# Reordered reads and weight splits in a gated attention kernel: the first tile's x on two queues, the border's x pieces in threes and twos

## The chip, the cores and the metric

The kernel runs on one core of a Trainium2 chip. The metric is the device time of one execution in microseconds (us), lower is better. Three timed runs of the kernel before gave 1965.87, 1967.68 and 1967.72 us; their median is 1967.68 us.

## What is computed

The reference takes x (2048 rows of 640), a key and a value cache of 32 heads (the last 512 positions of 128 are used), and weights in float32. It normalizes x, runs attention and a two-layer network on the same normalized rows, and gates the one with the other:

```python
xn = _layernorm(x, axis=-1)
s = _A_ref(xn, A_k_cache, A_v_cache, A_wq, A_wo)      # q = xn @ wq, softmax(q k^T / sqrt(128)) v, @ wo
g = _silu(_B_ref(xn, B_w1, B_b1, B_w2, B_b2))         # relu(xn @ w1 + b1)**2 @ w2 + b2
return x + s * g
```

The inner size of the network is 1728, that is 13 chunks of 128 and one of 64.

## The kernel before

Each float32 operand of a product is split into a high part (a rounded copy, made on ScalarE) and a low part (operand minus high part, made on VectorE or GpSimd), and each product of two operands takes three matmuls: high by high, high by low, low by high. "Preparing" a weight below means making these two parts.

**Tiles and stages.** The 2048 rows are four tiles of 512 columns (NT). In the first stage three tiles run through the network, one chunk f of its inner size after the other: `up` (L400), or `up_half` (L377) for the chunk of 64, makes one chunk of the hidden layer, and `down` (L426) adds its product with w2 to five banks of PSUM. The chunks are reordered so that the one of 64 stands at place rp = 3. The gates and the transposed normalized x are written to memory. In the second stage the 32 heads are worked off in 128 units: a half `hf` (two tiles), a group `g` of two heads, a tile t of the half, a head j of the group. Four units (UPG) make a group. The last tile's network follows behind the last units.

**The first tile.** `ln_first` (L208) normalizes the first 512 rows in four blocks of 128. SyncE (SP) issues the four reads of x (L222 to L225), then those of the first weights (`load_part`, L330), of the biases into `br`, and of the weights of chunks 1 and 2. Meanwhile TensorE runs WARM = 36 transposes of a constant (L242). For each block VectorE takes statistics (`bn`, two halves, then `aggr`); ScalarE takes roots (`root`), centres and scales the blocks; VectorE takes the reciprocal of the root, and GpSimd finishes that of the first two blocks (`newton(0)`). TensorE transposes the scaled blocks into `px` (`turn`), ScalarE and VectorE copy them to the two parts of `xT`, and `up` begins. `raws` holds the raw weights of chunk 0.

**Order within a chunk.** The engines work in the order in which the code records instructions. In tile 0, `square_split` (L369) squares the hidden chunk on GpSimd and then prepares w1 of chunk f + 1 (`split_w`, L359) ahead of splitting the hidden chunk itself.

**The order of the second stage** is a plan written out by hand: `at(when, f, ...)` (L964) notes a step with a due time, and L1150 records all steps sorted by time. A unit has PERIOD = 12.4 of that scale. The steps of a unit i that matter here:

- `s_mm` makes the scores in four banks `s`; `max_fold` and `gather` (three small ScalarE copies, at 3.95) and `row` (at 4.1) find the maximum of each column. `row` writes it as `rowm` to memory (`m_d`) and reads it back to all 128 partitions (`bm`), both DMAs on SP's queue, and the second is issued only when the first has landed.
- `shift` (at 10.4) subtracts `bm` from the four banks into `e` on VectorE, which frees the banks for the next unit's scores; `expo` and `p_hi` (ScalarE) and `p_lo` (GpSimd) make the parts `pt` for `v_mm`, the product with v.
- The sums take the same way back through `s_d` and `bs`.
- `r_mm` multiplies the outcome of both heads (`ot`) with wo into a running sum.
- Four weights of each group (q, k, v, o) are loaded into a raw tile, one of each kind, by `load_raw` on SP's queue and prepared by `prep` (ScalarE then GpSimd) one period later. L972 to L977 give the due times; each load is due 10.5 ahead of its own prep.
- At the border between the two halves, the second half's x is read: two tiles of ten pieces of 256 KB each (`load_xT`, L546; parts 0 and 1 of five chunks), at the times of X_AT (L984 to L994), all on ScalarE's DMA queue, over tiles that the first half's units have used.

In the notes below unit numbers count from 0; 64 is the first unit of the second half. L73 in the profile is the line of a helper that records most instructions, so the profile is read by tile names.

Of the kernel before, what the change touches and what calls it, by code (L numbers as in the profile page):

```python
# [14 lines left out]
P = 128  # L15
NT = 512
EPS = 1e-5
WARM = 36


@with_exitstack
def kernel(
# [15 lines left out]
    S, D = x.shape  # L38
# [3 lines left out]
    NB = NT // P  # L42
# [159 lines left out]
    def biases():  # L202
# [2 lines left out]
        dve.tensor_copy(b1_sb, pb[:, :FC])  # L205
        dve.tensor_copy(b2_sb, pb[:, 32 : 32 + DC])

    def ln_first():  # L208
        mv = xp.tile([P, 4, NB], F32, tag="mv", name="mv0")
        sc = xp.tile([P, 3, NB], F32, tag="sc", name="sc0")  # L210
# [5 lines left out]
        pool.memset(warm, 1.0)  # L216
        eps = mv[:, 3, 1:2]
        dve.memset(eps, EPS)
        act.activation(warm, warm, AF.Sqrt)
        hd = D // 2  # L220
        xn = []
        for b in range(NB):  # L222
            xb = ln_tile(0, b)
            sp.dma_start(xb, x[b * P : (b + 1) * P, :])
            xn.append(xb)  # L225
        br = xp.tile([P, P], F32, tag="br", name="br", bufs=1)
        dve.memset(br, 0.0)
        BR.append(br)
        for k in range(2):
            load_part(0, k)  # L230
        raws = [PRE[0, k] for k in range(2)]
        for lo, hi in ((0, rp), (rp, rp + 1), (rp + 1, FC)):
            f0, m = chunks[lo][0], chunks[lo][1]
            sp.dma_start(
                br[lo:hi, :m], b1[f0 : f0 + m * (hi - lo)].rearrange("(f p) -> f p", p=m)
            )
        sp.dma_start(br[32 : 32 + DC, :], b2.rearrange("(c p) -> c p", p=P))
        for f in (1, 2):
            for k in range(2):
                load_part(f, k)  # L240
# [11 lines left out]
        def aggr(b):  # L252
            dve.bn_aggr(mv[:, :2, b], sts[b])
# [29 lines left out]
        for b in range(n):  # L283
            for i in range(2):
                bn(b, i)
            aggr(b)
        centre(0)
        root(0)
        centre(1)
# [37 lines left out]
        for i in range(2):  # L327
            pool.dma_start(xT_d[t][i][:, cs, :], raw(xs[i])[:, cs, :])

    def load_part(f, k):  # L330
        f0, n = chunks[f]
        if f % 3 and f < 9:
            if k == 0:
                BOTH[f] = keep.tile([P, 2, D], F32, tag="acc", name=f"wr{f}", bufs=2)
            w = BOTH[f][:, k, :]
        else:
            w = xp.tile([P, D], F32, tag="stw", name=f"w{k + 1}r{f}", bufs=2)
        if k == 0:
# [30 lines left out]
    def square_split(t, f, r, hi, lo):  # L369
        g, a, v = engines(t)  # L370
        g.tensor_tensor(r, r, r, op=ALU.mult)
        if t == 0 and f:
            split_w(f + 1, 0)
        a.activation(hi, r, AF.Copy)
        v.tensor_tensor(lo, r, raw(hi), op=ALU.subtract)

    def up_half(t, f, xs):  # L377
        n = chunks[f][1]
        ph = ps_h.tile([P, NT], F32, tag="ph", name=f"ph{t}_{f}")
        w = w1s[f][0]  # L380
        order = [(c, i) for c in range(DC - 1) for i in range(2)] + [(DC - 1, 1), (DC - 1, 0)]
        for k, (c, i) in enumerate(order):
            m = n if i else 2 * n
            nc.tensor.matmul(
                ph[:m, :],
                w[:, c, :m],
                xs[i][:, c, :],
                start=k == 0,
                stop=k == len(order) - 1,
            )  # L390
        r = hp.tile([P, NT], F32, tag="r", name=f"r{t}_{f}")[:n, :]
        g, a, v = engines(t)
        a.activation(r, ph[n : 2 * n, :], AF.Copy)
        v.tensor_tensor(r, ph[:n, :], r, op=ALU.add)
        a.activation(r, r, AF.Relu, bias=b1_sb[:n, f : f + 1])
        h = hp.tile([P, NT], F32R, tag="h0", name=f"h{t}_{f}")
        square_split(t, f, r, h[:n, :], h[n : 2 * n, :])
        return h

    def up(t, f, xs):  # L400
        if chunks[f][1] < P:
            return up_half(t, f, xs)
        ph = ps_h.tile([P, NT], F32, tag="ph", name=f"ph{t}_{f}")
        if t == 0 and f < 2:
            order = [(c, i, j) for c in range(3) for i, j in ((0, 0), (0, 1))]
            order += [(0, 1, 0), (1, 1, 0), (3, 0, 0), (3, 0, 1), (2, 1, 0), (3, 1, 0)]
            order += [(4, 0, 0), (4, 1, 0), (4, 0, 1)]
        else:
            order = [(c, i, j) for c in range(DC) for i, j in ((0, 0), (0, 1), (1, 0))]
        for k, (c, i, j) in enumerate(order):  # L410
            nc.tensor.matmul(  # L411
                ph,
                w1s[f][i][:, c, :],
                xs[j][:, c, :],
                start=k == 0,
                stop=k == len(order) - 1,
            )
            if t == f == 0 and k == 9:
                biases()
        r = hp.tile([P, NT], F32, tag="r", name=f"r{t}_{f}")  # L420
        engines(t)[1].activation(r, ph, AF.Relu, bias=b1_sb[:, f : f + 1])
        hs = [hp.tile([P, NT], F32R, tag=f"h{i}", name=f"h{t}_{f}_{i}") for i in range(2)]
        square_split(t, f, r, hs[0], hs[1])
        return hs
# [542 lines left out]
    for n in range(HALF * NG):  # L967
        hf, g = divmod(n, NG)
        base = UPG * PERIOD * n
        for j in range(G):  # L970
            h = g * G + j
            for kind, when in (  # L972
                ("q", (j - 1 - AHEAD) * PERIOD + 8.4),
                ("k", (j - 2) * PERIOD + 8.5),
                ("v", j * PERIOD + 8.4),
                ("o", (j if n == 0 else -j) * PERIOD + 8.5),
            ):  # L977
                if n or kind in "vo":
                    at(base + when - 10.5, load_raw, kind, hf, h)
                    at(base + when, prep, kind, hf, h)  # L980
    at(10.0, pad, pools["ep"], 480)
    for t in range(TPH):
        w = (NG * UPG + t * G - 5) * PERIOD
        X_AT = [(11.65, 2)]  # L984
        for k in (1, 2):
            X_AT += [(k * PERIOD + 3.97, 2), (k * PERIOD + 7.85, 1)]
            X_AT += [(k * PERIOD + 11.65, 2)] * (k == 1)
        pieces = [(c, i) for c in range(DC) for i in range(2)]
        for k, (when, n) in enumerate(X_AT):
# [208 lines left out]
```

## Time and profile before

| what | value |
|---|---|
| time, median of three runs (lowest to highest) | 1967.68 us (1965.87 to 1967.72) |
| profiled execution, its own time | 1966.04 us |
| span of its program | 1964.2 us |
| mean granted TensorE clock | 0.998 |
| busy VectorE, ScalarE, GpSimd | 78%, 60%, 70% |
| DMA | 218.97 MB, mean 111 GB/s |

In a timeline row the first number is the start in us from the begin of the span, the second the duration, then come engine, line, operation, output<-inputs, shapes, the count of merged instructions, and in brackets the idle time of the engine just before, with what ended it. PE is TensorE's matmul, PEld its load of weights, DVE is VectorE, ACT ScalarE, POOL GpSimd; SPq and ACTq are the queues on which SyncE and ScalarE issue DMAs. A row of the windows view gives, for one stretch, its length, the busy time and count of each engine, the granted TensorE clock, the DMA share, and GB/s.

### The profile page before, as it was taken

To read this page: it belongs to the slowest core of one execution; us is meant where nothing else is said; L and a number is where in the kernel's file an instruction comes from. 1 tells how busy PE (TensorE), PEld (TensorE's weight loads), DVE (VectorE), ACT (ScalarE), POOL (GpSimd) and SP (SyncE) were. 2 spreads that over 40 slices of the span, in tenths; PEclk is the share of its full clock that TensorE was granted. 3 is DMA by queue.
4 is the path that set the end of the run, shared out by engine and by line. 5 is a ranking of instruction groups with operands and counts; after the bars stand their busy time and mean duration, and the time that the engine had idled before them with its cause. 6 is when DMAs were issued, how large, how long until landed. Compare 5 with 4: busy or idle time off the path is not lost. (4 is left out here: it accounts for less than half of the span.)

```text
span 1964.2 us, 25621 instructions
## 1 busy us (share of the span) xinstructions
PE 1952.7 (99%) x8612; PEld 1612.2 (82%) x8612; DVE 1535.0 (78%) x2640; ACT 1186.1 (60%) x2038; POOL 1375.1 (70%) x757
## 2 busy tenths in 40 slices
PE   9999999999999999999999999999999999999998
PEld 7888888888888888888887888888888888888887
DVE  5633337788888888888888878888888888888865
ACT  4432326766666666666666676666666666666643
POOL 2121226888878888888887888888888888888841
PEclk9999999999999999999999999999999999999999
DMA  5330453333333322222235433333333333323253
GB/s 181 95 118 28 182 198 128 97 92 92 92 92 92 92 92 93 92 91 94 90 95 181 133 119 108 113 113 113 113 113 113 113 113 114 97 92 92 86 187 118
DMA packets 127594, 218.97 MB, mean 111 GB/s; under 512 B 23420, under 2 KB 37542, under 8 KB 126182
## 3 DMA queue, kind: packets, MB, share of 16 engines
q1 hardware_dynamic: 121718, 197.67, 33.1%
q0 software_dynamic: 2864, 14.42, 1.8%
q10 hardware_dynamic: 2880, 5.24, 0.9%
q8 instruction: 67, 1.10, 0.2%
q14 instruction: 65, 0.53, 0.1%
HBM read 193.41 MB, written 23.87 MB: 111 GB/s over the span
## 5 line engine op out<-in xcount | busy, mean ns | idle before, releaser
L73 POOL TENSOR_TENSOR pt<-e,pt 128x1024 fp32r<-128x1024 f32 x256 | 615.2, 2403 | 125.6 <-ACT pt L73 99.1
L73 PE MATMUL r<-ot,wo 128*128 128x512 f32 x1920 | 496.7, 389 | 0.0
L73 PE MATMUL pq<-ax,wq 128*128 128x512 f32 x1920 | 456.1, 389 | 0.0
L73 PEld LDWEIGHTS pq<-ax,wq 128*128 128x128 f32 x1920 | 360.4, 188 | 75.2 <-DVE q L73 0.4
L73 PEld LDWEIGHTS r<-ot,wo 128*128 128x128 f32 x1920 | 360.4, 188 | 74.9
L73 PE MATMUL o<-pt,wv 128*128 128x512 f32 x1536 | 370.6, 390 | 0.2
L73 PE MATMUL s<-q,wk 128*128 128x512 f32 x1536 | 369.4, 389 | 1.1 <-DVE e L73 1.1
L73 ACT ACTIVATE e<-e 128x1024 f32<-128x1024 f32 x256 | 269.6, 1053 | 135.1 <-DVE e L73 110.2
L73 DVE TRANSPOSE_TENSOR_REDUCE rdm<-s 128x16 f32<-128x512 f32 x512 | 344.3, 709 | 6.3 <-PE s L73 6.3
L73 PEld LDWEIGHTS s<-q,wk 128*128 128x128 f32 x1536 | 288.1, 188 | 62.2 <-DVE e L73 2.4
L73 PEld LDWEIGHTS o<-pt,wv 128*128 128x128 f32 x1536 | 287.9, 188 | 62.0 <-POOL pt L73 2.6
L73 DVE TENSOR_TENSOR e<-s,bm 128x512 f32<-128x512 f32 x512 | 312.7, 666 | 16.6 <-DMA bm<-m_d 16.2
L73 POOL TENSOR_TENSOR su<-e,e 128x1024 f32<-128x1024 f32 x128 | 308.7, 2412 | 0.0
L73 ACT ACTIVATE pt<-e 128x1024 fp32r<-128x1024 f32 x256 | 271.9, 1062 | 8.2 <-ACT rdm L73 1.2
L73 DVE TENSOR_TENSOR acc<-r,acc 128x512 f32<-128x512 f32 x300 | 203.1, 677 | 10.6 <-PE r L73 10.4
L73 ACT ACTIVATE rdm<-rdm 32x64 f32<-32x64 f32 x384 | 97.7, 254 | 173.9 <-DVE rdm L73 170.7
L73 DVE TRANSPOSE_TENSOR_REDUCE rds<-su 128x32 f32<-128x1024 f32 x128 | 158.3, 1237 | 0.5 <-POOL su L73 0.5
L73 DVE TENSOR_TENSOR ot<-o,ot 128x512 fp32r<-128x512 f32 x128 | 88.5, 691 | 86.2 <-ACT ot L73 86.2
L73 ACT ACTIVATE q<-pq 128x512 fp32r<-128x512 f32 x128 | 76.6, 598 | 107.8 <-PE pq L73 107.8
L411 PE MATMUL ph<-xT,w1s 128*128 128x512 f32 x585 | 140.3, 391 | 0.1
L73 POOL TENSOR_TENSOR wq<-qr,wq 128x640 fp32r<-128x640 f32 x62 | 97.8, 1577 | 55.5 <-ACT wq L73 55.5
L73 POOL TENSOR_TENSOR wv<-vr,wv 128x512 fp32r<-128x512 f32 x64 | 83.1, 1298 | 71.4 <-ACT wv L73 64.3
(137 smaller groups left out, 1961.3 us busy)
## 6 DMA issues: line engine op xcount, KB each, us to landing
bm<-m_d SPq DMA_DIRECT2D x128, 256.0 KB, 3.3
bs<-s_d SPq DMA_DIRECT2D x128, 256.0 KB, 3.3
qr<-in_wq_dram SPq DMA_DIRECT2D x64, 320.0 KB, 4.8
or<-in_wo_dram SPq DMA_DIRECT2D x64, 320.0 KB, 4.1
kr<-in_kT_dram SPq DMA_DIRECT2D x64, 256.0 KB, 3.4
vr<-in_v_dram SPq DMA_DIRECT2D x64, 256.0 KB, 4.3
xT_d<-xT POOLq DMA_DIRECT2D x6, 1280.0 KB, 7.4
xb<-in_x_dram SPq DMA_DIRECT2D x16, 320.0 KB, 4.5
```

The costliest lines, as they stand in the source:

```text
L73: ins = method(*args, **kwargs)
L411: nc.tensor.matmul(ph, w1s[f][i][:, c, :], xs[j][:, c, :], start=k == 0, stop=k == len(order) - 1,)
```

## The change

It has four parts.

1. *First tile's reads.* The first block of x is read in two halves of 320 columns, one on SP's queue and one on ScalarE's; block 1 and 3 follow on SP's queue, block 2 on ScalarE's, whose two issues now stand ahead of its first activation. The reads of the first weights, the biases and the weights of chunks 1 and 2 move into a function `first_reads` that is called behind the first block's `aggr`; the first of them is tied to VectorE's work by a write of one column into its tile (`held`), so it and all that stands behind it on SP's queue wait for that. WARM goes from 36 to 40.
2. *Splits of chunks 4 and 5.* In tile 0, w1 of chunk 4 is prepared ahead of the hidden chunk 3's first copy instead of behind its square, and w1 of chunk 5 ahead of hidden chunk 4's Relu.
3. *Weight order.* The due times of the preps change by up to 0.13, so that in three of a group's four units the two weights prepared there (and their two loads) change places: q before v, k before q, o before k.
4. *Border.* A tile's ten pieces of x are read in four groups of two and three: two on SP's queue just behind unit 59's `bm`, three on ScalarE's just behind unit 60's `gather`, two on SP's behind unit 60's `bm`, three on ScalarE's behind unit 61's `gather`; the second tile the same two units later. Before they were groups of 2, 2, 1, 2, 2 and 1, all on ScalarE's queue, at three places in a unit's course.

```diff
-WARM = 36
+WARM = 40
...
+    def first_reads(br):
+        for k in range(2):
+            load_part(0, k, k == 0)
...
+        return [PRE[0, k] for k in range(2)]
...
-        act.activation(warm, warm, AF.Sqrt)
-        hd = D // 2
-        xn = []
-        for b in range(NB):
-            xb = ln_tile(0, b)
-            sp.dma_start(xb, x[b * P : (b + 1) * P, :])
-            xn.append(xb)
+        hd = D // 2
+        xn = [ln_tile(0, b) for b in range(NB)]
+        for i, q in enumerate((sp, act)):
+            js = slice(i * hd, (i + 1) * hd)
+            q.dma_start(xn[0][:, js], x[:P, js])
+        for b in range(1, NB):
+            (sp if b % 2 else act).dma_start(xn[b], x[b * P : (b + 1) * P, :])
+        act.activation(warm, warm, AF.Sqrt)
...
             aggr(b)
+            if b == 0:
+                raws = first_reads(br)
...
-    def load_part(f, k):
+    def load_part(f, k, held=False):
...
             w = xp.tile([P, D], F32, tag="stw", name=f"w{k + 1}r{f}", bufs=2)
+            if held:
+                dve.memset(w[:, :1], 0.0)
...
-        if t == 0 and f:
+        if t == 0 and f not in (0, rp, rp + 1):
             split_w(f + 1, 0)
...
         g, a, v = engines(t)
+        if t == 0:
+            split_w(f + 1, 0)
         a.activation(r, ph[n : 2 * n, :], AF.Copy)
...
         r = hp.tile([P, NT], F32, tag="r", name=f"r{t}_{f}")
+        if t == 0 and f == rp + 1:
+            split_w(f + 1, 0)
...
-                ("q", (j - 1 - AHEAD) * PERIOD + 8.4),
-                ("k", (j - 2) * PERIOD + 8.5),
+                ("q", (j - 1 - AHEAD) * PERIOD + (8.42 if j else 8.35)),
+                ("k", (j - 2) * PERIOD + (8.5 if j else 8.37)),
                 ("v", j * PERIOD + 8.4),
-                ("o", (j if n == 0 else -j) * PERIOD + 8.5),
+                ("o", (j if n == 0 else -j) * PERIOD + 8.45),
...
-        X_AT = [(11.65, 2)]
-        for k in (1, 2):
-            X_AT += [(k * PERIOD + 3.97, 2), (k * PERIOD + 7.85, 1)]
-            X_AT += [(k * PERIOD + 11.65, 2)] * (k == 1)
+        X_AT = ((4.3, 2, sp), (PERIOD + 3.97, 3, act))
+        X_AT += ((PERIOD + 4.3, 2, sp), (2 * PERIOD + 3.97, 3, act))
...
-                at(w + when, load_xT, 1, t, i, slice(c, c + 1), act)
+                at(w + when, load_xT, 1, t, i, slice(c, c + 1), queue)
```

More of the change, by code (lines that the diff above doesn't have):

```diff
@@ L206, in biases @@
         dve.tensor_copy(b2_sb, pb[:, 32 : 32 + DC])
+    def first_reads(br):
+        for k in range(2):
+            load_part(0, k, k == 0)
+        for lo, hi in ((0, rp), (rp, rp + 1), (rp + 1, FC)):
+            f0, m = chunks[lo][0], chunks[lo][1]
+            sp.dma_start(
+                br[lo:hi, :m], b1[f0 : f0 + m * (hi - lo)].rearrange("(f p) -> f p", p=m)
+            )
+        sp.dma_start(br[32 : 32 + DC, :], b2.rearrange("(c p) -> c p", p=P))
+        for f in (1, 2):
+            for k in range(2):
+                load_part(f, k)
+        return [PRE[0, k] for k in range(2)]
     def ln_first():
@@ L228, in ln_first @@
         BR.append(br)
[L229 to L240, printed above, removed]
         pw = psx.tile([P, NT], F32, tag="x", name="pw")
@@ L983 @@
         w = (NG * UPG + t * G - 5) * PERIOD
-        X_AT = [(11.65, 2)]
-        for k in (1, 2):
-            X_AT += [(k * PERIOD + 3.97, 2), (k * PERIOD + 7.85, 1)]
-            X_AT += [(k * PERIOD + 11.65, 2)] * (k == 1)
+        X_AT = ((4.3, 2, sp), (PERIOD + 3.97, 3, act))
+        X_AT += ((PERIOD + 4.3, 2, sp), (2 * PERIOD + 3.97, 3, act))
         pieces = [(c, i) for c in range(DC) for i in range(2)]
-        for k, (when, n) in enumerate(X_AT):
+        for k, (when, n, queue) in enumerate(X_AT):
             if k == 0:
```

## The prediction

> **What bounds the kernel.** I read the page first: its span, its busy line and one of its costliest groups.
>
> ```profile
> span 1964.2 us, 25621 instructions
> PE 1952.7 (99%) x8612; PEld 1612.2 (82%) x8612; DVE 1535.0 (78%) x2640; ACT 1186.1 (60%) x2038; POOL 1375.1 (70%) x757
> L73 PE MATMUL s<-q,wk 128*128 128x512 f32 x1536 | 369.4, 389 | 1.1 <-DVE e L73 1.1
> ```
>
> TensorE is busy for all but 11.5 us of the span, and its 8612 matmuls set the end. One takes 0.389 us from start to end, but they overlap: twelve take 2.88 us in the row at 1035.44 below, so one starts every (2.88 - 0.39) / 11 = 0.227 us. No edit adds or takes work there (four transposes apart), so the change is worth what it takes from TensorE's waits, or adds to them. I then read the timeline of the first 16 us, all engines, rows of one line each.
>
> ```profile
> 0.75 1.28 ACT L73 ACT_TABLE_LOAD   x1 [0.75 <-PEq L1181]
> 0.76 1.82 SPq L73 DMA_DIRECT2D xb<-in_x_dram  x4
> 0.82 0.06 DVE L73 MEMSET mv<- 128x1 f32 x1 [0.82 <-PEq L1181]
> 1.38 5.52 PE L73 MATMUL pw<-ident 128*128 128x128 f32 x36 [1.38 <-POOL mv L73]
> 2.61 0.43 SPq L73 DMA_DIRECT2D w1r<-in_w_dram  x1
> 3.71 0.89 DVE L73 BATCH_NORM_STATS2 st<-xb 128x6 f32<-128x320 f32 x2 [2.66 <-DMA xb<-in_x_dram]
> 4.75 0.83 DVE L73 BATCH_NORM_STATS2 st<-xb 128x6 f32<-128x320 f32 x2
> 5.87 0.30 ACT L73 ACTIVATE sc<-mv 128x2 f32<-128x2 f32 x1 [0.17 <-DVE mv L73]
> 6.82 2.95 SPq L73 DMA_DIRECT2D wr<-in_w_dram  x4
> 6.83 0.49 DVE L73 BATCH_NORM_STATS2 st<-xb 128x6 f32<-128x320 f32 x1 [0.79 <-DMA xb<-in_x_dram]
> 7.24 0.15 DVE L73 RECIPROCAL sc<-sc 128x2 f32<-128x2 f32 x1
> 8.53 0.83 ACT L73 ACTIVATE xb<-xb,mv 128x640 f32<-128x640 f32 x1 [1.65 <-POOL mv L73]
> 9.41 3.93 PE L73 MATMUL px<-ident,xb 128*128 128x128 f32 x20 [2.52 <-ACT xb L73]
> 10.17 0.73 ACT L73 ACTIVATE w1s<-w1r 128x640 fp32r<-128x640 f32 x1
> 11.67 2.56 ACT L73 ACTIVATE xT<-px 128x512 fp32r<-128x512 f32 x5 [0.78 <-PE px L73]
> 13.00 3.25 PE L411 MATMUL ph<-xT,w1s 128*128 128x512 f32 x10
> ```
>
> The network's first matmul (`ph`) starts at 13.00. Follow it back: `px` transposes from 9.41, which wait for ScalarE's scaling at 8.53, which waits for GpSimd's roots, which start with VectorE's reciprocal at 7.24. ScalarE had made its square root by 6.17 (5.87 + 0.30). The reciprocal stands behind the first half statistic of block 2 (6.83, 0.79 us idle until x landed). So block 2 of x sets the head. The windows view of the same stretch shows how full the DMA engines are, and the clock:
>
> ```profile
> 0.00:2.00 2.00, 0.62 (x3) 0.63 (x4) 0.22 (x2) 1.25 (x1) 0.75 (x7) 1.00 0.16 15
> 2.00:4.00 2.00, 2.00 (x12) 2.00 (x11) 0.29 (x1) 0.23 (x2) 0.00 (x0) 1.00 0.93 329
> 12.00:14.00 2.00, 2.00 (x10) 1.80 (x9) 1.70 (x3) 2.00 (x5) 1.64 (x2) 0.50 1.01 378
> ```
>
> The DMA share is 0.93 at 329 GB/s while x is read: x's reads are at the engines' rate, and the weights (issued from 2.61) stand among them. In the third row the granted clock is 0.50: the first ten `ph` take 3.25 us, where ten at full clock take 9 x 0.227 + 0.39 = 2.43, so 0.8 us is lost there.
>
> The second place is the network's chunks 4 and 5, in TensorE's weight loads and ScalarE's rows:
>
> ```profile
> 37.36 2.86 PEld L411 LDWEIGHTS ph<-xT,w1s 128*128 128x128 f32 x13 [0.51 <-DVE w1s L73]
> 43.28 2.82 PEld L411 LDWEIGHTS ph<-xT,w1s 128*128 128x128 f32 x13 [0.34 <-DVE w1s L73]
> 35.41 0.72 ACT L73 ACTIVATE w1s<-wr 128x640 fp32r<-128x640 f32 x1
> 41.33 0.73 ACT L73 ACTIVATE w1s<-wr 128x640 fp32r<-128x640 f32 x1
> ```
>
> TensorE waits 0.51 and 0.34 us for VectorE's low part of w1, whose high part ScalarE began only at 35.41 and 41.33, behind the hidden chunk's Relu.
>
> The third is the border between the halves, in the first score matmuls of units 60, 61 and 65:
>
> ```profile
> 1035.44 2.88 PE L73 MATMUL s<-q,wk 128*128 128x512 f32 x12
> 1048.46 3.05 PE L73 MATMUL s<-q,wk 128*128 128x512 f32 x12 [0.62 <-DVE e L73]
> 1099.29 2.88 PE L73 MATMUL s<-q,wk 128*128 128x512 f32 x12
> ```
>
> Units 60 to 65 are five steps. A step is 54 matmuls (15 for q, 12 scores, 12 with v, 15 with wo), undisturbed 54 x 0.2267 = 12.24 us, so 61.2; the rows are 63.85 apart. **The border loses 2.65 us.** Why, in SyncE's and ScalarE's queues, and VectorE:
>
> ```profile
> 1028.12 0.33 SPq L73 DMA_DIRECT2D m_d<-rowm  x1
> 1029.46 0.33 SPq L73 DMA_DIRECT2D bm<-m_d  x1
> 1040.37 0.32 SPq L73 DMA_DIRECT2D m_d<-rowm  x1
> 1043.51 0.33 SPq L73 DMA_DIRECT2D bm<-m_d  x1
> 1039.12 0.33 ACTq L73 DMA_DIRECT2D ax<-xT_d  x1
> 1039.49 0.44 ACTq L73 DMA_DIRECT2D ax<-xT_d  x1
> 1043.12 0.33 ACTq L73 DMA_DIRECT2D ax<-xT_d  x1
> 1047.71 2.48 DVE L73 TENSOR_TENSOR e<-s,bm 128x512 f32<-128x512 f32 x4 [2.09 <-DMA bm<-m_d]
> ```
>
> Unit 59's maximum (`m_d`, issued 1028.12) is back for the next DMA 1.34 us later. Unit 60's takes 3.14 us: two pieces of x (`ax`, 256 KB each) were issued about a microsecond before it. `bm` then goes out 0.4 us behind a third piece and is used 4.2 us later; `shift` waits 2.09 us for it, and TensorE's scores wait for `shift` (0.62 in the row at 1048.46). From `m_d`'s issue to `shift` it took 7.34 us.
>
> **The change part by part.** The profiled execution took 1966.04 us, 1.84 more than its span; the median of the runs is 1.64 us above it, and the lowest run 0.17 below it. I sum savings against the profiled execution and take the same sum off the median.
>
> *Head: 0.4 us saved (between -0.2 and 0.8).* SP's four issues took 1.82 us, 0.455 each; now SP issues three and ScalarE two at the same time. The bytes are the same, and the share says that the engines, not the issues, are the limit: by 2.0 hardly anything has come (15 GB/s up to there), so three blocks, 0.98 MB at 329 GB/s, are there 3.0 us later, at 5.0, and I add 0.3 for landing: blocks 1 and 2 share the engines and land together, near 5.2. Block 1's statistics thus start 0.45 later than now (4.75), but block 2's no longer wait. The sum: 5.2 + 0.83 statistics + 0.29 to the root (5.87 - 4.75 - 0.83) = 6.32, root until 6.62, the half statistic of block 2 (0.49) until 6.85, reciprocal at 6.85 instead of 7.24: 0.4 saved. If the blocks come as late as block 2 does now, minus the held weights' share, nothing or -0.2; if block 1 keeps its place and only the wait of 0.79 goes, 0.8. All of what follows (roots, scaling, `px`, `xT`) waits on this chain and moves with it. The new memset is 0.06 (row at 0.82), on this chain, counted in -0.2. ScalarE's two issues (0.455 each) delay its table load, which ends at 2.03 now and would end near 3; the root at 5.87 needs it: nothing. WARM's four extra transposes lie in the 2.52 us in which TensorE waits for `px`: nothing.
>
> The held weights are issued near 4.9 instead of 2.61. The raw w1 is needed by ScalarE at 10.17 - 0.4 = 9.8 and may come as late as 10.5 (0.73 before the copies to `xT`, at 11.3 then). From issue to landing it now takes at most 10.17 - 2.61 = 7.6, behind all of x; with x nearly done, I take 3 to 4 us, so 8 to 9: nothing lost. The biases and chunk 1's and 2's weights queue behind it on SP: the last four go out from near 7.1 instead of 6.82, and none is used ahead of chunk 0's own.
>
> *Chunks 4 and 5: 0.6 us saved (0.4 to 0.8).* The two waits are 0.51 and 0.34, 0.85 together; a little of each lies between any two loads, so I take 0.6. The splits move ahead of work that waits for TensorE anyway. What is late next is the hidden chunk's own split, which has a whole `up` of 3.4 us (15 x 0.227) of room.
>
> *Border: 2.3 us saved of 2.65 (1.0 to 2.65).* No piece goes out between `m_d` and `bm` any more; those on SP's queue stand behind `bm`. Three instead of two go out before `m_d`. With two ahead, `m_d` took 3.14 instead of 1.34, with late weights in the queue as well; I take an extra 1.2 for three, between 0 and 2. `bm` alone takes 1047.71 - 1043.51 = 4.2 at most and (this row has a piece 0.39 ahead of it) I take 3.4. So 1.34 + 1.2 + 3.4 = 5.9 from `m_d` to `shift`, against 7.34; and as 7.34 costs TensorE 0.8 (1048.46 - 1035.44 - 12.24 = 0.78), 6.6 costs nothing. At the high end, 1.34 + 2 + 4.2 = 7.5, nothing is saved in that unit; the lower bound lets this hold in half of them. Behind SP's pieces stand the sums' write (`s_d`) and then weights; the write has a queue of at most two pieces ahead of it, as now. The third issue holds ScalarE 0.33 to 0.44 us longer (rows at 1039.12 and 1039.49) ahead of a `p_hi` whose `p_lo` stands behind `s_add` on GpSimd; without that cover it would cost up to 0.4 in each of four units. SP's first piece waits until TensorE has left the old x; what stands behind it is that same write, due later.
>
> *Weight order: nothing.* All four kinds of prep remain, one behind the other on ScalarE and GpSimd; each pair takes as long as before, and each weight is used at least a unit (12.24 us) later. What could go wrong is the second rival.
>
> **Sum: 0.4 + 0.6 + 2.3 = 3.3 us.** The profiled execution would become 1962.7; the median 1967.68 - 3.3 = 1964.4, that is 0.17% less.
>
> [...]
>
> **The rivals.** *The clock stays up.* After `pw` TensorE idles 2.52 us, then works in pieces, and the clock is 0.50 when `ph` begins. With four more transposes (5.52 / 36 = 0.15 each on the average, 0.6) and `px` 0.4 earlier, the gap shrinks to about 1.5. If that keeps the clock, 0.8 more is saved: 4.1, or 1963.6. For it speaks that the drop follows the gap; against it, that the trace has no gap of 1.5 to compare. [...]
>
> *The new weight order stalls ScalarE: slower.* In one unit of four, o's prep now comes first, and its tile is freed only by the last `r` matmuls just before:
>
> ```profile
> 738.23 0.63 ACT L73 ACTIVATE wk<-kr 128x512 fp32r<-128x512 f32 x1
> 738.77 0.72 ACT L73 ACTIVATE wo<-or 128x640 fp32r<-128x640 f32 x1
> 736.24 1.52 PE L73 MATMUL r<-ot,wo 128*128 128x512 f32 x6
> ```
>
> ScalarE comes to this pair at 738.23, `r` ends at 737.76. So 0.47 us is left; beyond that, ScalarE's stall reaches `pt`, and with 32 groups each 0.25 us beyond it costs 8.0: it decides from a wait of 0.47, and with 0.25 more gives 1967.68 - 3.3 + 8.0 = 1972.4. Against it: both ends hang on the same TensorE order, and the head doesn't shift them against each other.
>
> *The border is not cured* (three pieces push `m_d` as far as two and a third did) and the head gives nothing: 0.6 of chunks 4 and 5 remain, and half a microsecond of the border: 1.1, or 1966.6.
>
> **How the numbers follow.** A change under 0.2% (3.9 us: below 1963.74 is faster, above 1971.6 slower) is about what a measurement of this kernel can't tell from none. Forecast 0.50; clock up 0.25; border not cured 0.19; slower 0.06. The forecast lies 0.7 above the lower bound and the clock case 0.1 below it; the runs before differ by 1.85, and the mean of the four executions shown (1966.83) is 0.85 under the median, which leans both to the low side. I count 0.18 of the forecast's 0.50 and 0.20 of the clock's 0.25 as faster. Faster 0.38, same 0.32 + 0.05 + 0.19 = 0.56, slower 0.06. The range goes from 1962.0 (full clock, 4.1 less than the profiled execution's 1966.04) to 1967.5 (border not cured, and a median 0.9 higher).
>
> **What would show it.** Right: the reciprocal near 6.85 and `ph` near 12.6; no wait of PEld for w1 in chunks 4 and 5; the scores of units 60 and 65 under 62 us apart; from `m_d` to `shift` under 6.4 in units 60 to 63. Wrong: block 1's statistics after 5.6, the raw w1 landing after 10.5, `m_d` over 3 us with three pieces ahead, or TensorE idle between units 4 and 59 beside ScalarE's o.

## The result, and the profile after

The changed kernel took 1969.31 us (median of 21 runs, 1968.37 to 1970.39), the kernel before 1966.12 beside it (21 runs, 1964.41 to 1968.14): ratio 1.0016, 95% interval 1.0009 to 1.0022. So it is 3.2 us slower (1.8 to 4.3), where 3.3 us less had been forecast. The profiled execution has a span of 1966.6 us, against 1964.2.

The page of the changed kernel, its span and its busy line (busy time of each engine, share, instructions):

```profile
span 1966.6 us, 25644 instructions
PE 1954.2 (99%) x8616; PEld 1612.0 (82%) x8616; DVE 1533.8 (78%) x2641; ACT 1186.7 (60%) x2038; POOL 1376.7 (70%) x757
```

TensorE's work is the same, four transposes apart, so again only its waits can differ. The timeline of the head:

```profile
4.78 0.38 SPq L73 DMA_DIRECT2D w1r<-in_w_dram  x1
5.15 0.89 DVE L73 BATCH_NORM_STATS2 st<-xb 128x6 f32<-128x320 f32 x2 [0.42 <-DMA xb<-in_x_dram]
6.40 0.49 DVE L73 BATCH_NORM_STATS2 st<-xb 128x6 f32<-128x320 f32 x1
6.80 0.15 DVE L73 RECIPROCAL sc<-sc 128x2 f32<-128x2 f32 x1
8.98 0.77 PE L73 MATMUL px<-ident,xb 128*128 128x128 f32 x5 [0.38 <-ACT xb L73]
12.03 2.13 PE L420 MATMUL ph<-xT,w1s 128*128 128x512 f32 x6
```

The chain came as it was worked out: block 1's statistics at 5.15 (forecast 5.2), block 2's without a wait, the reciprocal at 6.80 (6.85). `ph` starts 0.97 us earlier than in the profiled execution of before. Chunks 4 and 5, TensorE's weight loads:

```profile
35.68 3.36 PEld L420 LDWEIGHTS ph<-xT,w1s 128*128 128x128 f32 x15
41.34 3.36 PEld L420 LDWEIGHTS ph<-xT,w1s 128*128 128x128 f32 x15
```

Fifteen loads in one row, no wait for `w1s`: the 0.51 and 0.34 us are gone. Up to here the change is ahead. Now the start of the second stage, first in the kernel before (`eu` is the first layer of the last tile's network, parts of which run early, between the first units):

```profile
297.33 0.84 PE L73 MATMUL eu<-xT,w1s 128*128 128x512 f32 x3
305.65 0.33 SPq L73 DMA_DIRECT2D m_d<-rowm  x1
307.14 0.33 SPq L73 DMA_DIRECT2D bm<-m_d  x1
312.97 2.88 PE L73 MATMUL s<-q,wk 128*128 128x512 f32 x12
```

and in the changed one:

```profile
295.93 2.43 PE L73 MATMUL eu<-xT,w1s 128*128 128x512 f32 x10
304.26 0.32 SPq L73 DMA_DIRECT2D m_d<-rowm  x1
307.74 0.33 SPq L73 DMA_DIRECT2D bm<-m_d  x1
311.77 2.48 DVE L73 TENSOR_TENSOR e<-s,bm 128x512 f32<-128x512 f32 x4 [4.79 <-DMA bm<-m_d]
312.61 3.01 PE L73 MATMUL s<-q,wk 128*128 128x512 f32 x12 [0.87 <-DVE e L73]
```

From the first `eu` matmul to the scores of unit 1 it now takes 16.68 us instead of 15.64: unit 0's maximum was away for 3.48 us instead of 1.49, and TensorE waits 0.87 us for `shift`. No step of the prediction touched this place. The border:

```profile
1034.53 2.88 PE L73 MATMUL s<-q,wk 128*128 128x512 f32 x12
1060.52 3.01 PE L73 MATMUL s<-q,wk 128*128 128x512 f32 x12 [0.82 <-DVE e L73]
1074.88 3.05 PE L73 MATMUL s<-q,wk 128*128 128x512 f32 x12 [1.45 <-DVE e L73]
1100.78 1.52 PE L73 MATMUL s<-q,wk 128*128 128x512 f32 x6
...
1066.56 0.33 SPq L73 DMA_DIRECT2D m_d<-rowm  x1
1070.21 0.33 SPq L73 DMA_DIRECT2D bm<-m_d  x1
1074.13 2.48 DVE L73 TENSOR_TENSOR e<-s,bm 128x512 f32<-128x512 f32 x4 [2.31 <-DMA bm<-m_d]
```

Units 60 to 65 now lie 66.25 us apart instead of 63.85: the border loses 5.05 us. Unit 62's `m_d` took 3.65 and `shift` followed it by 7.57.

### The profile page after: what moved, and what is told of

It reads as the page before. It is cut to its first block, busy times and chain, and to the rows that moved or that the text cites. A ratio compares the mean times of both kernels' runs of the same rounds, so it can differ in the third digit from the quotient of the medians.

```text
span 1966.6 us, 25644 instructions
## 1 busy us (share of the span) xinstructions
PE 1954.2 (99%) x8616; PEld 1612.0 (82%) x8616; DVE 1533.8 (78%) x2641; ACT 1186.7 (60%) x2038; POOL 1376.7 (70%) x757
## 5 line engine op out<-in xcount | busy, mean ns | idle before, releaser
L73 ACT ACTIVATE rds<-rds 32x32 f32<-32x32 f32 x384 | 89.7, 234 | 70.0 <-DVE rds L73 66.6
L420 PEld LDWEIGHTS ph<-xT,w1s 128*128 128x128 f32 x585 | 109.5, 188 | 23.4 <-DVE xT L73 0.9
```

Of the source, the lines that this page charges most:

```text
L73: ins = method(*args, **kwargs)
L420: nc.tensor.matmul(ph, w1s[f][i][:, c, :], xs[j][:, c, :], start=k == 0, stop=k == len(order) - 1,)
```

## The experiments

Theory, from these two traces: the change loses at the border, through the pieces ahead of `m_d`, and something at the start of the second stage eats what the head gained. Rivals: the new weight order, the head's shift against the gate's stores (the head's change moves unit 0's maximum into the time in which the gates are written to memory), or one lucky and one unlucky execution.

The table holds all kernels: ratio to the kernel before with its interval (11 runs each, 21 for the whole change), then, from the one profiled execution of each, the start of the first `ph`, `m_d`'s trip in unit 0 (issue of `m_d` to issue of `bm`), first `eu` to the scores of unit 2, and scores of unit 60 to those of 65 (61.2 undisturbed).

| kernel | ratio, 95% | `ph` | unit 0 | `eu` to unit 2 | 60 to 65 |
|---|---|---|---|---|---|
| before | 1 | 13.00 | 1.49 | 27.53 | 63.85 |
| whole change | 1.0016 (1.0009 to 1.0022) | 12.03 | 3.48 | 28.98 | 66.25 |
| e1 head | 1.0003 (0.9994 to 1.0011) | 12.32 | 3.32 | 28.45 | 63.69 |
| e2 splits | 0.9996 (0.9987 to 1.0005) | 11.74 | 1.51 | 27.52 | 64.33 |
| e3 border | 1.0004 (0.9995 to 1.0012) | 11.55 | 1.49 | 27.52 | 65.17 |
| e4 weight order | 0.9999 (0.9991 to 1.0008) | 11.89 | 1.58 | 27.52 | 63.33 |
| e5 head, 36 | 1.0001 (0.9992 to 1.0010) | 11.95 | 1.67 | 27.52 | 65.98 |
| e6 before, 40 | 1.0005 (0.9996 to 1.0014) | 12.33 | 3.53 | 28.95 | 64.17 |
| e7 whole, old border | 1.0006 (0.9997 to 1.0014) | 12.56 | 3.03 | 28.53 | 63.51 |
| e8 splits, 3 and 2 behind `bm` | 1.0000 (0.9991 to 1.0008) | 11.99 | 1.49 | 27.52 | 64.69 |
| e9 whole, 36 | 1.0003 (0.9994 to 1.0012) | 12.10 | 1.46 | 27.52 | 65.68 |
| e10 border, 2 ahead | 1.0006 (0.9997 to 1.0015) | 11.73 | 1.50 | 27.52 | 65.83 |
| e11 border, ScalarE's cut | 0.9989 (0.9980 to 0.9998) | 12.68 | 1.50 | 27.52 | 61.22 |
| e12 border, SyncE's cut | 0.9994 (0.9985 to 1.0003) | 12.73 | 1.49 | 27.53 | 63.85 |
| g1 whole again | 1.0013 (1.0004 to 1.0022) | 12.41 | 3.33 | 28.80 | 64.91 |
| g2 splits, even | 0.9993 (0.9984 to 1.0002) | 12.81 | 1.50 | 27.52 | 63.78 |
| g3 whole, 36, even | 1.0003 (0.9995 to 1.0012) | 12.16 | 1.46 | 27.52 | 65.76 |
| g4 splits, GpSimd's queue | 1.0002 (0.9993 to 1.0011) | 11.96 | 1.61 | 27.53 | 64.17 |
| g5 splits, 4 behind `bm` | 1.0004 (0.9994 to 1.0013) | 11.96 | 1.49 | 27.52 | 65.05 |

### The four parts alone

**e1**, the head's part of the diff on the kernel before (WARM 40, `first_reads`, x over two queues, held weights).

> The head's part alone on the kernel before (first reads on two queues, first weights held, 40 warm transposes). Theory (the loss of the whole change lies at the border, and the head keeps what it gained up to the first down matmuls): about 1.0 us less than the kernel before, 1965.1; the first `ph` near 12.0 to 12.6 and the clock not halved behind 11. Rival A (the head's shift brings unit 0's maximum into the gate's stores, so that the second stage's start loses what was gained): 0.5 to 1 us more than before, 1966.6 to 1967.1, with the first shift of unit 0 more than 7 us behind its `m_d`. Rival B (the head gives nothing outside of one lucky execution): 1966.1.

**e2**, the moved `split_w` calls of chunks 4 and 5 alone. (The expectation names chunk 1 as well; its split stays where it was.)

> The moved weight splits of chunks 1, 4 and 5 alone on the kernel before. Theory: the two waits of TensorE near 37 and 43 us go, 0.5 to 0.6 us less than before, 1965.5. Rival: a new wait of 0.3 us near 20 us and a later one take it back: 1966.0.

**e3**, the new `X_AT` with its queues alone.

> The border's pieces alone (threes on ScalarE's queue at the gather, twos on SyncE's behind the broadcast) on the kernel before. Theory: the border loses 5.0 us instead of 2.65, since `m_d` stands 3 us behind three pieces in all four units and the sums' write stands behind two more: 2.4 us more than before, 1968.5; the scores of units 60 and 65 lie over 65.5 us apart. Rival (the border's loss comes from the swapped weight order, which puts other weights behind the pieces, and not from the pieces): 1966.1 or less, under 64 us apart.

**e4**, the new due times of the weights' `prep` alone.

> The order of the weight splits alone on the kernel before. Theory: no change, 1966.1 (between 1965.7 and 1966.5), no TensorE wait over 0.1 us between units 4 and 59. Rival (the new order costs at the start of the second stage, where unit 0's maximum and the first loads stand, and at the border): 1.4 to 2.2 us more, 1967.5 to 1968.3.

None of the four is told from no change by its ratio; the profiles say more. e4 has neither unit 0's long trip nor the border's greater loss, so that rival is gone. But the weight order is not quite free. In all six profiles with the new order a 16 KB packet of instructions (the next section says what these are) starts 0.3 to 0.6 us behind the issue of unit 95's `m_d`. That trip then takes 2.3 to 2.6 us, and the step behind it is 0.1 to 0.6 longer, 0.3 on the mean; none of the thirteen profiles with the old order has the packet there, and none loses more than 0.03 in that step. e2 gains its 0.6: from the first `ph` to the last `py` it takes 283.67 us, and between 283.62 and 283.68 in all ten kernels with the splits, against 284.10 to 284.30 in the nine without. e3's border loses 3.97, less than the 5.0 expected. And e1 alone brings unit 0's long trip, where a gain of 1.0 us had been expected. The head itself is a surprise: in e2, e3 and e4 the old head starts `ph` at 11.55 to 11.89, over a microsecond ahead of the profiled execution of before.

### Four transposes

In the changed kernel, the view of the DMA queues between the issue of unit 0's `m_d` and that of `bm` (packets, MB, share of 16 engines) has a queue that the kernel before does not have there. Changed, 304.2 to 307.8:

```profile
q8 instruction: 1, 0.02, 1.7%
q14 instruction: 1, 0.01, 0.9%
q1 hardware_dynamic: 48, 0.00, 0.8%
```

before, 305.6 to 307.2:

```profile
q14 instruction: 1, 0.01, 1.9%
q1 hardware_dynamic: 48, 0.00, 1.6%
```

A 16 KB packet of instructions (q8) moves before `m_d` is back; in the kernel before it came 8.1 us behind the issue. The same view in shorter windows shows what it does. In the kernel before, all 48 tiny packets of `m_d` have moved 1.2 us behind its issue. In the changed one 45 have, and the last three move 1.3 us later (304.2 to 305.4, then 306.6 to 306.8):

```profile
q1 hardware_dynamic: 45, 0.00, 2.1%
```

```profile
q1 hardware_dynamic: 3, 0.00, 2.2%
```

The trace has the 16 KB packet from 1.46 to 2.44 us behind the issue, and the three at 2.43 to 2.45: they stand behind it. In the other four profiles with 40 transposes it is the same, three of 48, at the end of the 16 KB packet.

Over the span there are 67 of these packets, one for every 128 or so matmuls. Count TensorE's instructions (matmuls, weight loads and, over the span, some 85 others) that have started when a packet starts: in all nineteen profiles and for all 67 packets, numbered from 0, it is 256 for each packet ahead of it, plus 150 to 220. So they go by TensorE's own instructions. The head's part adds four transposes to TensorE, and also one DMA; e5 and e6 tell these apart.

**e5** and **e6**, each one line, e5 on e1 and e6 on the kernel before:

```
e5  -WARM = 40      e6  -WARM = 36
    +WARM = 36          +WARM = 40
```

> The head's part alone with 36 warm transposes instead of 40. In the head's part alone, unit 0's `m_d` took 3.32 us instead of 1.5, with a 16 KB packet of an instruction queue 0.9 us behind its issue; in the kernel before that packet came 8.1 us behind it. Theory F (the four added transposes move the place at which TensorE's instructions are fetched, and the fetch holds the small write up): with 36 the packet is away from `m_d` again, `m_d` of unit 0 takes about 1.5, `shift` follows 5.4 behind it, and the kernel is about 1.0 us faster than the head's part with 40: 1964.9. Rival L (the added first read or the held weights move it, by one more DMA ahead): the packet stays within 2 us of `m_d`, which takes 3.3; 1965.9.

> The kernel before with 40 warm transposes instead of 36 and nothing else. Theory F (the count of TensorE's instructions sets where their fetch falls): unit 0's `m_d` takes over 3 us with a 16 KB instruction packet in it, the second stage starts 1.0 us later against the first `eu` matmul, about 1.0 us slower than before: 1966.3 with the before of the last four runs (1965.1). Rival L (one more DMA ahead moves it, not the transposes): `m_d` at 1.5, no change, 1965.1.

SyncE's rows and the scores of e6, whose only edit is the number:

```profile
305.15 0.32 SPq L73 DMA_DIRECT2D m_d<-rowm  x1
308.68 0.33 SPq L73 DMA_DIRECT2D bm<-m_d  x1
313.47 3.00 PE L73 MATMUL s<-q,wk 128*128 128x512 f32 x12 [0.84 <-DVE e L73]
```

The trip is 3.53, TensorE waits the 0.84 that it waits in the whole change, and from `eu` to unit 2 it takes 28.95. Theory F holds and Rival L falls. It holds over the whole table: in the five profiles with 40 transposes the 16 KB packet comes 0.9 to 1.5 us behind `m_d`'s issue, the trip is 3.03 to 3.53 and the scores of unit 2 come 0.9 to 1.5 us late; in the fourteen with 36 the packet comes 4.1 to 9.3 us behind it, the trip is 1.46 to 1.67, and `eu` to unit 2 is 27.52 or 27.53. Units 111 and 85 follow the same line: their trips are 1.33 to 1.37 in all fourteen with 36; with 40 unit 111's is 2.58 to 3.08 in all five, unit 85's 3.03 to 3.08 in four. Unit 111 of the changed kernel, and the matmuls with v that wait in the end:

```profile
1669.28 0.33 SPq L73 DMA_DIRECT2D m_d<-rowm  x1
1671.88 0.32 SPq L73 DMA_DIRECT2D bm<-m_d  x1
1675.01 2.48 DVE L73 TENSOR_TENSOR e<-s,bm 128x512 f32<-128x512 f32 x4 [0.79 <-DMA bm<-m_d]
1686.61 1.43 PE L73 MATMUL o<-pt,wv 128*128 128x512 f32 x5 [0.40 <-POOL pt L73]
```

The step behind unit 111 is 0.3 to 0.9 us longer for it in the five profiles with 40, the one behind unit 85 0.2 in the four with the long trip. So four transposes cost some 2.0 us at these three places: 1.2 on the mean at the start, 0.8 later. (Units 2 to 60 take 709.5 us on the mean with 40 and 709.9 with 36; single profiles reach from 709.2 to 711.6, so this 0.3 in favour of 40 is not counted.) The whole time of e6 (1.0005) is by itself not told from no change.

Not every meeting costs: a packet meets unit 45's `m_d` in all nineteen profiles, whose trip takes 2.5 to 3.2 us, and the step behind it is at most 0.2 longer.

**e9**, the whole change with `WARM = 36`, and **g1**, the whole change again, each beside the kernel before.

> The whole change with 36 warm transposes instead of 40. Theory F (four more transposes move the fetch of TensorE's instructions into unit 0's `m_d`): unit 0's `m_d` near 1.5 instead of 3.48, the second scores come 15.6 us behind the first `eu` instead of 16.7, and the third scores another 0.4 us earlier: 1.0 to 1.4 us less than the whole change, so about 2 us above the kernel before instead of 3.2. Rival (the loss of the start of the second stage comes from the head's shift against the gate's stores): unit 0 as in the whole change, 3.2 above. At the border the loss stays at 4.0 to 5.1.

> The whole change again, with its 40 transposes. Theory F: unit 0's `m_d` takes over 3 us with a 16 KB instruction packet in it; 2 to 3 us over the kernel before. Rival (the first comparison of the whole change fell on a worse chip or hour): less than 1 us over it.

e9 is at 1.0003, g1 at 1.0013 with its interval above 1: the loss is the change's, no matter of the first comparison, and with 36 transposes no loss can be told any more. e9's profiled execution is a late one all the same (span 1966.7): there the packet met unit 3's `m_d` (3.19 us), and the steps of units 3 and 4 lost 1.5 us. Only in e9's profile does a packet start behind the issue of unit 3's `m_d`; the meetings in units 0 and 111 are in all five profiles with 40 transposes.

### The border

**e7**, the whole change with the old `X_AT`.

> The whole change without the border's part (the pieces of x as in the kernel before). Theory (of the 3.2 us lost, the border's pieces hold 1.4 to 2.4, the head's later start and unit 0's wait the rest, the splits give 0.6 back): 1.4 to 2.4 us less than the whole change, 1966.2 to 1967.0 where the kernel before is at 1966.1 (0.1 to 0.9 above it); the scores of units 60 and 65 lie 63.3 to 64.4 us apart, as in the four kernels with the old pieces. Rival (the new order of weights makes the border worse, whatever the pieces): over 65 us apart and 2 us or more above the kernel before.

The border is back at 63.51, and the ratio at 1.0006: the new weights' order does nothing to it. In the seven profiles with the old pieces the border takes 63.3 to 66.0, 64.1 on the mean; in the four with the new ones 64.9 to 66.3, mean 65.5. So the new pieces cost 1.4 more on the mean, of single executions that scatter by up to 2.7.

**e8**, on e2, no piece ahead of `m_d`:

```
+X_AT = ((4.3, 3, sp), (11.65, 2, act), (PERIOD + 4.3, 3, sp), (PERIOD + 11.65, 2, act))
```

> The splits' part with other places for x's pieces: three on SyncE's queue right behind the broadcast, two on ScalarE's behind the first half's exponents, none between the previous unit's sums and `m_d`. Theory (what costs at the border is pieces in front of `m_d`; the same bytes behind `bm` are covered): `m_d` takes 1.4 to 1.7 in units 60 to 63, `shift` follows it by 5.2 to 6.0, the scores of units 60 and 65 are 61.2 to 62.0 apart, about 2 us less than the splits alone: 2.5 us under the kernel before. Rival B (any 1.25 MB a unit in those units costs as much, since the broadcast, the sums' trip and the weights share the engines): over 63.5 apart, no gain over the splits alone (0.8 under the kernel before).

A miss: 64.69 apart, `m_d` 3.04 in unit 60. Five pieces behind `bm` held the sums' `s_d` up for 4.95 us, with it `bs` and the weights behind `bs`, and the weights were still moving when the next `m_d` was issued.

**e10**, on the kernel before, two ahead and three behind:

```
+X_AT = ((4.3, 3, sp), (PERIOD + 3.97, 2, act))
+X_AT += ((PERIOD + 4.3, 3, sp), (2 * PERIOD + 3.97, 2, act))
```

> The border's part alone, with two pieces on ScalarE's queue at the gather instead of three, and three on SyncE's queue behind the broadcast instead of two. Theory P (pieces ahead of `m_d` set its trip, about 0.9 us for each: 3.0 with three, 2.2 with two in the kernels so far): `m_d` 2.0 to 2.4 in units 60 to 63, the scores of units 60 and 65 under 63.8 apart, no slower than the kernel before. Rival W (all the bytes of a unit count: what goes behind the broadcast delays the sums' trip, and with it the weights, into the next `m_d`): `m_d` about 3 again and 65 us or more apart, 0.6 us over the kernel before.

Again 65.83, `m_d` 2.58 to 3.04. Theory P in its simple form, so much for each piece, falls. **e11** and **e12** take bytes away instead of moving them. They leave out seven eighths of the columns of some pieces, and the second half's x takes the first half's tiles (`XT[1, t] = XT[0, t]`), so the second half computes with old values there. Both are e3 with this and

```
+m = NT // 8 if hf and queue is act else NT      # e12: queue is sp
 queue.dma_start(raw(XT[hf, t][i])[:, cs, :m], xT_d[hf * TPH + t][i][:, cs, :m])
```

> The border's part alone, with the three pieces at the gather cut to an eighth of their columns (the issues stay; the second half computes with the old values in the columns left out, and writes the new ones into the old tiles). Theory P: `m_d` 1.4 to 1.8 in units 60 to 63, the scores of units 60 and 65 at most 62 us apart, 3 us less than the border's part and 2 us less than the kernel before. Rival W: `m_d` stays over 2 in most of these units, since the weights stand in front of it, and the border loses over 2 us.

> The border's part alone, with the two pieces behind the broadcast cut to an eighth of their columns (as above, for SyncE's queue). Theory P: `m_d` stays near 3.0, since three pieces stand ahead of it, and `shift` follows by 6.0 to 6.6 because the broadcast is alone; the border loses 1.5 to 3 us. Rival W: the sums' write is back in 1.4 us, the weights are in before `m_d`, which takes about 2.2; the border loses under 1.5 us.

e11's scores of units 60 and 65, and unit 61's last piece and maximum:

```profile
1034.34 2.88 PE L73 MATMUL s<-q,wk 128*128 128x512 f32 x12
1095.56 2.88 PE L73 MATMUL s<-q,wk 128*128 128x512 f32 x12
...
1051.11 0.49 ACTq L73 DMA_DIRECT2D ax<-xT_d  x1
1051.50 0.33 SPq L73 DMA_DIRECT2D m_d<-rowm  x1
1053.21 0.33 SPq L73 DMA_DIRECT2D bm<-m_d  x1
```

61.22 apart: without the three pieces' bytes the border loses nothing, although their issues and SyncE's two pieces are still there; 0.9989 is the only ratio whose interval lies below 1. With SyncE's pair cut instead (e12) `m_d` stays at 2.9 to 3.13 in all four units, but `shift` follows by 6.0 to 6.4, and 2.65 is lost. Both kernels use the first half's tiles, so that alone does not cure the border. The bytes ahead of `m_d` carry the larger part: without them nothing is left of e3's 3.97, without those behind `bm` 2.65 is. These are single profiles.

**g2**, on e2, and **g3**, on e9: all twenty pieces on SyncE's queue, two behind `bm` and two behind `bs` in each of units 59 to 63.

> The splits' part with x's pieces spread evenly over units 59 to 63, all on SyncE's queue: two behind the broadcast, two behind the second sums' broadcast and a weight, 36 transposes, no head's part, no new weight order. Theory P (pieces that still move when `m_d` is issued are what costs; two behind the broadcast are covered): `m_d` 1.4 to 2.3 in units 60 to 63, the scores of units 60 and 65 at most 62.3 us apart, 2 us or more under the kernel before. Rival W (the second pair and the weights behind it are still on their way when `m_d` is issued, in every unit): `m_d` about 3, over 64 apart, at most 0.8 us under the kernel before, as the splits alone.

> The whole change with 36 transposes and the evenly spread pieces of the kernel beside it. Theory: the head's part loses 0.3 to 0.6 us against the old head (blocks 0 and 1 share the engines), the rest as beside it, so 1.5 to 2 us under the kernel before. Rival W as beside it: within 0.5 us of the kernel before.

g2 loses 2.58 at the border with `m_d` at 2.0 to 3.0, g3 4.56: spreading does not cure it. g2's ratio is the lowest of the kernels that do all the work, but it is not told from 1. **g4**, on e2, has the pieces on GpSimd's queue (`(6.5, 3, pool), (PERIOD + 1.4, 2, pool)` and so on); **g5**, on e2, four pieces behind `bm` on SyncE's.

> The splits' part with x's pieces issued by GpSimd, three behind the second `pt` of a unit and two behind its weights' low parts, where it is idle for 0.6 to 1.5 us; the same bytes over the same units. Theory Q (`m_d` waits for packets of its own queue): `m_d` 1.4 to 1.9 in units 60 to 63 with pieces of the other queue on their way, the scores of units 60 and 65 under 62.5 apart, 2 us or more under the kernel before. Rival W (the engines are full, whatever the queue): `m_d` 2 to 3, over 63.5 apart, at most 1 us under. Rival G (0.54 us a piece on GpSimd delays the next `pt`): `m_d` near 1.4 and yet over 63.5 apart, with TensorE waiting for `pt`.

> The splits' part with all of x's pieces on SyncE's queue behind the broadcast, four in each of units 59 to 63. Theory T (`m_d` lands with the last transfer issued ahead of it): the sums' trip behind four pieces takes 3.5 to 4.5 us instead of 1.3, the weights behind it land 1 to 2 us into the next `m_d`, which therefore takes 1.8 to 2.6 and lands within 0.3 us of the second weight; the scores of units 60 and 65 62.5 to 63.5 apart, 1.2 to 2.2 us under the kernel before. Rival (pieces count only as many as are issued ahead of `m_d`; with none, `m_d` is free): `m_d` 1.34 to 1.6, under 62 apart. Rival W (same bytes, same loss): over 64 apart, at most 0.8 under.

The tile views of the transfers issued last ahead of an `m_d` give their time from issue to landing, where the trace has the landing. g5's second weight in unit 61, and the `m_d` behind it:

```profile
L73 SPq DMA_DIRECT2D kr<-in_kT_dram x1: 422/422/422, 1061.1 to 1061.1; - x1
DMA to landing us min/median/max: 5.8/5.8/5.8
```

```profile
1064.24 0.32 SPq L73 DMA_DIRECT2D m_d<-rowm  x1
1067.08 0.33 SPq L73 DMA_DIRECT2D bm<-m_d  x1
```

The weight lands at 1066.9, `bm` goes out at 1067.08. In the kernel before, ScalarE's second piece ahead of unit 60's `m_d`:

```profile
L73 ACTq DMA_DIRECT2D ax<-xT_d x2: 327/386/444, 1039.1 to 1039.5; - x2
DMA to landing us min/median/max: 3.9/3.9/3.9
```

1039.49 + 3.9 = 1043.4, and `bm` at 1043.51. In g4's unit 62, GpSimd's two pieces, and SyncE's rows:

```profile
L73 POOL DMA_DIRECT2D ax<-xT_d x2: 546/554/563, 1060.4 to 1060.9; - x2
DMA to landing us min/median/max: 5.8/6.2/6.6
```

```profile
1063.58 0.33 SPq L73 DMA_DIRECT2D m_d<-rowm  x1
1067.72 0.33 SPq L73 DMA_DIRECT2D bm<-m_d  x1
```

1060.9 + 6.6 = 1067.5, and `bm` at 1067.72. That is Theory T: `m_d` is back about 0.2 us behind the last transfer issued ahead of it, a piece or a weight, whether SyncE or ScalarE issued it. In units 60 to 63 of all nineteen profiles the landing of that transfer is known 29 times, and in 23 of them it is so (0.17 to 0.23 us). It is not so with three whole pieces ahead, the last of them issued 0.1 to 0.4 us before `m_d`. Unit 63 of the changed kernel, its third piece and its maximum:

```profile
L73 ACTq DMA_DIRECT2D ax<-xT_d x1: 443/443/443, 1080.5 to 1080.5; - x1
DMA to landing us min/median/max: 3.7/3.7/3.7
```

```profile
1080.93 0.33 SPq L73 DMA_DIRECT2D m_d<-rowm  x1
1083.84 0.34 SPq L73 DMA_DIRECT2D bm<-m_d  x1
```

The piece lands at 1084.2, `bm` is out at 1083.84. In the five kernels with these pieces `m_d` is back 0.2 to 0.4 us ahead of the third piece there, and 0.8 to 1.2 behind the second in units 60 and 61: **it waits for what is well under way when it is issued, not for all that was issued ahead.** (The 29th is g4's unit 63, 0.6 behind a piece that landed 1.0 after the issue of `m_d`.) With the last weight nearly through it took 1.34 (g4's unit 61) to 1.43 (g5's). g5 got its shorter `m_d` in units 60, 61 and 63 (2.44, 1.43, 1.99), but `bm` with four pieces behind it took 4.2 to 4.6 to `shift` there, and 65.05 came of it. In g4 a weight of SyncE's own queue was issued in the same microsecond as that piece, and its landing is not in the trace: whether GpSimd's queue alone would let `m_d` pass stays open. It helped nothing.

A small write's own packets are late: with nothing ahead (unit 59 of the kernel before) they move 0.82 to 0.98 us behind the issue of `m_d`, in unit 60, among the packets of ScalarE's pieces, 1.5 to 2.7, and in unit 0 of the changed kernel three of them move at 2.43 to 2.45, when the 16 KB packet ends. From the end of the last of them to the issue of `bm` it takes 0.34 us in unit 59, 0.42 in unit 60 and 1.01 in unit 0; why it is longer there, no run here shows.

## Why the prediction was wrong

- **Where it failed first: "WARM's four extra transposes lie in the 2.52 us in which TensorE waits for `px`: nothing."** Their time does. But they move all of TensorE's later instructions, and with them the place where a block of these is fetched, into the `m_d` of units 0, 85 and 111: some 2.0 us (alone in e6, undone in e5 and e9). In unit 111 the packet moves by 0.4 to 1.4 us, about the time of four matmuls (0.9). In units 0 and 85 it moves by 2.6 to 8.4: by the count at which it comes with 40 it would be due, with 36, some 2 to 3 us behind the issue of `m_d`, when `bm` is already out, and it comes at 4.1 to 9.3. That `bm` and what follows it keep it back is a reading; no run tests it.
- **Border, "1.34 + 1.2 + 3.4 = 5.9 from `m_d` to `shift`".** The largest miss: 2.3 saved was forecast, 1.4 more lost (mean of four against seven profiles) was measured. From `m_d` to `shift` it took 6.4 to 7.6 in the changed kernel. The extra of `m_d` was 1.6 to 2.3, not 1.2: it waits for the second piece and for a good part of the third, which is issued only 0.3 to 0.4 us ahead of it. `bm` with two pieces behind it took 3.5 to 3.9, not 3.4. And "6.6 costs nothing" was wrong too: unit 63's 6.36 goes with a step of 13.15 us, 0.9 too long, since the delay passes on to `pt`, for which the matmuls with v wait as well. That a unit could save nothing was said; that the loss grows was not: the lower bound and the third rival both stopped at a saving. The step "the write has a queue of at most two pieces ahead of it, as now" left out what follows it: `bs` and the weights go later, and become what the next `m_d` waits for (e8, g5).
- **Head, 0.4 saved.** The new chain was right to 0.05 us in the profiled execution (the 0.3 us that it adds for landing stands in no row; the blocks were there at 5.15, against 5.2). The base was not: 13.00 is the latest of twelve starts of `ph` with the old head. These lie between 11.55 and 13.00, mean 12.20; the seven of the new head between 11.95 and 12.56, mean 12.22. So nothing is saved on the average. Block 2's wait of 0.79 belonged to that execution; in e2 block 2 is not waited for, in g2 1.12 us.
- **Clock.** The rival came true, the clock stays at 1.00 after the change, and was worth nothing: the profiled execution of before is the only one of nineteen in which it drops; the old head keeps it in eleven others, behind a gap of 2.17 us too (g2). The price was wrong as well: with the clock at 1.00 the first ten `ph` take 3.06 to 3.08 us in the other eighteen, not 2.43, so the drop cost 0.2 there, not 0.8. And the execution with the drop took 284.10 us from `ph` to the last `py`, the least of the nine without the splits, so that was had back.
- **Chunks 4 and 5, 0.6.** Right: 0.6 in ten profiles against nine.
- **Weight order, nothing.** Nearly right: 0.3 in unit 95, by a packet of instructions and not by a stall of ScalarE. The slower rival did not come true.

By the profiles' stages the whole change is then 2.0 for the transposes, plus 1.4 for the border, plus 0.3 for the weight order, minus 0.6 for the chunks, plus 0 for the head: 3.1 us slower. The two comparisons say 3.2 and 2.6, with intervals from 0.8 to 4.3. The split rests on the profiles: the ratios of the four parts, e1 to e4, are each too near 1 to be told from it, and together they come to 1.0002.

## What to carry to other kernels

In this kernel a small write that is read back waited for the bulk transfers that were under way when it was issued: `m_d` took 1.34 us in unit 59 of the changed kernel and 2.9 to 3.65 in units 60 to 63. Count what is still moving then, weights too. Reordering bytes within the same microseconds did not mend such a place here (63.78 to 65.83 us for units 60 to 65 in e3, e8, e10, g2, g4 and g5); taking bytes away did (61.22), in a kernel that leaves them out (e11), and no run shows it in one that does all the work. That the time of an added instruction is hidden did not make it free here: four transposes on the bounding engine cost some 2.0 us at other places. Look at the instruction queues in the DMA view beside each short round trip, before and after. And a wait read from one profiled execution near a start-up is a sample: take several profiles before a term is built on it.

## What the runs showed of the hardware that was not expected

- Fetching instructions is traffic that a small write waits for: one 16 KB packet of 0.9 to 1.3 us held three of the 48 packets of a 2 KB write, and made its trip of 1.5 us one of 3.0 to 3.5. The packets come one for every 256 of TensorE's instructions (67 in 17309 of the kernel before).
- The start of the first `ph` of one unchanged head scatters by 1.45 us (11.55 to 13.00), the border's loss by 2.7 (63.3 to 66.0 for the old pieces). Both together are more than the change was worth.
- Three pieces of 256 KB in each of four units cut to an eighth (e11) gave 2.8 us in the medians (interval of the ratio 0.4 to 3.9 us), about the border's whole loss in the profiled execution of before (2.65).
